# K transposed on VectorE in 32x32 word blocks, q block-diagonal and stationary, pairs of both batches in 16 KB rows

## The chip and the metric

One core of a Trainium2 chip. The metric is the device time of one execution in microseconds; the time before is the median of three runs. The profile shows one execution, taken by the hardware profiler. Engines: TensorE (PE; PEld is its weight load), VectorE (DVE), ScalarE (ACT), GpSimd (POOL) and SyncE (SP), which here only issues transfers; 16 DMA engines move the data.

## What is computed

One decoding step of attention over a sliding window, gated by a small dense block. Cut to what matters:

```python
# x: 2 x 1 x 448; k_cache, v_cache: 2 x 8 x 8192 x 256; wq: 448 x 4096; wo: 4096 x 448; all bf16
xn = layernorm(x)
q = (xn @ wq).reshape(2, 1, 16, 256)            # 16 query heads on 8 K/V heads
k, v = the last 2048 rows of k_cache, v_cache   # per batch and head
p = softmax(q @ k.T * 256 ** -0.5)
s = (p @ v).reshape(2, 1, 4096) @ wo
g = silu(relu(xn @ w1) @ w2)                    # w1: 448 x 1792, w2: 1792 x 448
return x + s * g
```

K and V are 2 x 8 x 2048 x 256 elements each, 16 MB each; wq and wo are 3.5 MB each, w1 and w2 1.5 MB each. Each byte is used once, for one row of q per head, so nearly all the kernel does is to bring K and V in and to turn them into the layout that TensorE wants.

## The kernel before

A pair `k` is one K/V head with both batches (8 pairs); a half is one batch of it, `c = 2k + b`. A half of K or V is one transfer of 1 MB, 128 rows of 8 KB: partition p holds 16 consecutive positions. There are 6 buffers for halves of K and 8 for V.

For the scores the contraction runs over the 256 head elements, so these must lie on partitions, while the transfer puts positions there. `do_T` (L262) therefore transposes K: it reads two bf16 elements as one 4-byte word, transposes four blocks of 128 x 128 words on TensorE into one of three PSUM banks (`tb`), and the bank is copied to a `kt` buffer, by VectorE (L280) and ScalarE (L282) in turn. A pair has 8 such steps. `do_S` (L284) makes the scores of a batch in 8 matmuls with q stationary (4 columns: even or odd head elements, the two heads of the pair) and 512 positions of `kt` streaming, four at a time in column strips of TensorE (`tile_position`). Their lines show as L249, the helper `mm`.

The softmax of a pair: `ch_max` (L300) takes row maxima on VectorE; `ch_rmT` (L305) brings them into one row on TensorE and takes the maximum per head (L309); `ch_bias` (L313) spreads it back over partitions; `ch_exp` (L319) is the exponential on ScalarE with the row sums; `ch_Pt` (L324) transposes P in four TensorE steps and a copy; `ch_sum` (L336) adds the row sums on TensorE with a reciprocal behind it. `do_PV` (L341) multiplies P, stationary in 4 columns, by V, four matmuls of 256 columns at a time. `do_osb` (L355) scales, on VectorE; `do_oT` (L361) turns the result onto partitions and writes it to `at_exp`. At the end `at_exp` is turned into `at2`, 128 small matmuls with `wo` follow (L491), then the gate, the residual and two stores.

The order of work is written out by hand: `steps` is a table of 64 steps, one per `do_T`, into which everything else is put at fixed distances (`at_step`, L435). Every engine executes its own list in that order and waits on semaphores where an operation names what it depends on; so an operation that waits holds all behind it on its engine. The transfers are SP's list, in a fixed order: two halves of K, wq, w1, w2, two halves of K, then V and K in turn (`order`, L462), and wo in five pieces (`WO_PARTS`); a load waits until the transposes (K) or the matmuls (V) that read its buffer last are done. `do_q`, `do_H`, `do_hT` and `do_F` (query, dense block and gate) run once, among the first steps.

## Time and profile before

| | |
|---|---|
| runs | 114.83, 115.55, 116.62 us (median 115.55) |
| profiled execution | 114.63 us, its span 112.8 us |
| busy | PE 81.9, DVE 49.5, ACT 44.5, POOL 1.8 us |
| moved | 44.24 MB, on average 392 GB/s |
| mean granted TensorE clock | 0.884 |

The span goes from the first to the last instruction. The slices of the page cut it in 40 equal parts; PEclk is the clock that TensorE was granted, in tenths, and GB/s is what the transfers moved. The groups of the page and of the view by line give the count of a kind of instruction, its busy time in total and the mean of one in ns, then the idle time of its engine ahead of it and who ended that. The chain that ended last follows the work back from the last instruction, at each step to what released it.

### The profile page before, as it was taken

Reading aid. Unit: us, or ns where it says so; the run is one execution under the profiler, and the core shown is the slowest. Engines: PE = TensorE matmul, PEld = TensorE weight load, DVE = VectorE, ACT = ScalarE, POOL = GpSimd, SP = SyncE. Lnnn points to the kernel's source line nnn. Section 1 sums busy time; section 2 is a strip of 40 time slices with the busy share of each in tenths; the row PEclk is TensorE's granted clock in tenths of the full one; section 3 lists DMA queues with packets and bytes.
Section 4 is the critical chain, followed back from the end, with each engine's and each line's share of the span. In section 5 each row is a group of like instructions: output and inputs, shape, how many; then the busy total and the mean of one; then the engine's idle time right before and its main releaser. Section 6 shows DMA issues by size and latency. Waiting matters only on the chain.

```text
span 112.8 us, 2285 instructions
## 1 busy us (share of the span) xinstructions
PE 81.9 (73%) x990; PEld 51.8 (46%) x990; DVE 49.5 (44%) x131; ACT 44.5 (39%) x57; POOL 1.8 (2%) x13
## 2 busy tenths in 40 slices
PE   0008966005978799999959948998999998675770
PEld 0008952002425476665636526654756664342640
DVE  2038333101125765755826724373665575534201
ACT  0960770000340475666643570367357465020000
POOL 6000000000000000000000000000000000000000
PEclk9999999855589999999999998599999999975555
DMA  2999989999999999999999999999999999999910
GB/s 67 418 483 427 478 346 422 425 423 418 433 412 421 424 418 424 412 421 418 421 418 427 421 418 418 415 421 418 427 415 418 427 424 418 416 422 426 359 58 4
DMA packets 5933, 44.24 MB, mean 392 GB/s; under 512 B 674, under 2 KB 932, under 8 KB 1316
## 3 DMA queue, kind: packets, MB, share of 16 engines
q1 hardware_dynamic: 5896, 44.11, 94.1%
q8 instruction: 7, 0.11, 0.4%
q14 instruction: 2, 0.02, 0.0%
q10 hardware_dynamic: 28, 0.00, 0.0%
HBM read 44.11 MB, written 0.00 MB: 391 GB/s over the span
## 4 chain that ended last, share of the span: by engine, by line
DMA 67%; PE 22%; DVE 4%; SPq 3%; issue 1%; ACT 0%
DMA kbuf<-in_A_k_cache_dram 43%; DMA wqo<-in_A_wo_dram 24%; PE tb L270 9%; PE fbk L249 6%; SPq L36 3%; PE sbk L249 3%; PE obk L249 2%; DVE h_n L406 1%; PE mbk L249 1%; PE mbk L327 1%; DVE tmp L429 1%; DVE kt L280 1%; DVE rm L301 1%; PE mbk L306 0%; DVE tmp L496 0%
## 5 line engine op out<-in xcount | busy, mean ns | idle before, releaser
L270 PE MATMUL tb<-ident_f,kbuf 128*128 128x128 f32 x256 | 43.6, 307 | 10.8 <-DMA kbuf<-in_A_k_cache_dram 10.8
L282 ACT ACTIVATE kt<-tb 128x1024 bf16<-128x1024 bf16 x32 | 32.8, 1024 | 43.8 <-PE tb L270 43.7
L270 PEld LDWEIGHTS tb<-ident_f,kbuf 128*128 128x128 f32 x256 | 31.7, 156 | 19.0 <-DMA kbuf<-in_A_k_cache_dram 11.7
L280 DVE COPY kt<-tb 128x1024 bf16<-128x1024 bf16 x32 | 22.0, 689 | 23.4 <-PE tb L270 23.4
L249 PE MATMUL obk<-vbuf,pt 128*4 128x256 bf16 x256 | 13.0, 292 | 0.0
L249 PE MATMUL sbk<-kt,qz 128*4 128x512 bf16 x128 | 10.4, 401 | 0.0
L357 DVE TENSOR_SCALAR o_sb<-obk,rs 128x256 bf16<-128x256 f32 x16 | 7.5, 471 | 1.6 <-PE obk L249 1.6
L301 DVE TENSOR_REDUCE rm<-sbk 128x1 f32<-128x512 f32 x8 | 5.5, 690 | 5.9 <-PE sbk L249 5.9
L320 ACT ACTIVATE e_sb<-sbk,bias 128x512 bf16<-128x512 f32 x8 | 5.5, 683 | 3.7 <-DVE bias L316 3.7
L249 PE MATMUL mbk<-ident,xg 2*128 2x2 bf16 x7 | 0.3, 163 | 8.9 <-DVE xg L229 8.9
L249 PEld LDWEIGHTS obk<-vbuf,pt 128*4 128x4 bf16 x256 | 4.3, 84 | 5.4 <-issue 3.2
L249 PE MATMUL fbk<-w_sb,xr 128*4 128x448 bf16 x14 | 4.1, 451 | 0.7 <-DVE h_n L406 0.7
L249 PEld LDWEIGHTS mbk<-ident,xg 2*128 2x128 bf16 x7 | 0.3, 100 | 8.9 <-DVE xg L229 8.9
L249 PE MATMUL fbk<-wqo,at 128*2 128x112 bf16 x128 | 3.6, 294 | 0.9 <-issue 0.4
L249 PE MATMUL mbk<-ssum,gsum 128*128 128x1 f32 x16 | 3.2, 270 | 0.6 <-DVE pt L332 0.6
L406 DVE TENSOR_SCALAR h_n<-fbk 4x448 bf16<-4x448 f32 x2 | 1.2, 612 | 5.4 <-PE fbk L249 5.4
L332 DVE COPY pt<-mbk 128x64 bf16<-128x64 bf16 x8 | 1.5, 192 | 4.6 <-PE mbk L327 4.6
L249 PEld LDWEIGHTS fbk<-wqo,at 128*2 128x2 bf16 x128 | 2.8, 118 | 1.6 <-issue 0.6
L327 PE MATMUL mbk<-ident,e_sb 128*128 128x128 bf16 x32 | 3.2, 222 | 0.3 <-ACT e_sb L320 0.3
L249 PEld LDWEIGHTS mbk<-ssum,gsum 128*128 128x128 f32 x16 | 2.7, 212 | 1.3 <-DVE pt L332 0.9
L249 PEld LDWEIGHTS mbk<-one_f,mrow 1*128 1x128 f32 x16 | 2.3, 182 | 2.0 <-DVE mrow L309 2.0
L249 PE MATMUL mbk<-one_f,mrow 1*128 1x1 f32 x16 | 3.0, 256 | 0.3 <-DVE mrow L309 0.3
(65 smaller groups left out, 43.9 us busy)
## 6 DMA issues: line engine op xcount, KB each, us to landing
kbuf<-in_A_k_cache_dram SPq DMA_DIRECT2D x16, 1024.0 KB, 23.0
vbuf<-in_A_v_cache_dram SPq DMA_DIRECT2D x16, 1024.0 KB, 25.2
wqo<-in_A_wq_dram SPq DMA_DIRECT2D x1, 3584.0 KB, 15.0
w_sb<-in_B_w_dram SPq DMA_DIRECT2D x2, 1568.0 KB, 19.7
wqo<-in_A_wo_dram SPq DMA_DIRECT2D x2, 1120.0 KB, 24.3
wqo<-in_A_wo_dram SPq DMA_DIRECT2D x1, 896.0 KB, 27.1
wqo<-in_A_wo_dram SPq DMA_DIRECT2D x2, 224.0 KB, 24.7
x_c<-in_A_x_dram ACTq DMA_DIRECT2D x2, 0.9 KB
```

The lines of the kernel that those rows point to most:

```text
L36: o = _Op(eng, lambda e: e.dma_start(dst, src), [d for d in deps if d is not None], True)
L249: return lambda e: e.matmul(out_ap, lhsT=lhsT, rhs=rhs, start=start, stop=stop, skip_group_check=True, **kw)
L270: o = pr.op(PE, lambda e, n=n, lo=lo: e.matmul(bank_f[:, n * 128:(n + 1) * 128], lhsT=src_f[:, lo:lo + 128], rhs=ident_f[:, :], start=True ...
L280: evac[i] = pr.op(DVE, lambda e: e.tensor_copy(dst[:, :], bank[:, :]), deps)
L282: evac[i] = pr.op(ACTE, lambda e: e.activation(dst[:, :], bank[:, :], ACT.Copy), deps)
L301: st["rm", k] = pr.op(DVE, lambda e: e.tensor_reduce(out=rm[k % 2][:, :], in_=sbk[:, :], axis=AX.X, op=ALU.max), [st["S", k], st.get(("rmT ...
L320: st["exp", k] = pr.op(ACTE, lambda e: e.activation(e_sb[k % 2][:, :], sbk[:, :], ACT.Exp, bias=bias[k % 2][:, 0:1], accum_out=ssum[k % 2] ...
L327: o = pr.op(PE, lambda e, j=j: e.matmul(mb16[:, 512 + 128 * j:640 + 128 * j], lhsT=e_sb[k % 2][:, 128 * j:128 * j + 128], rhs=ident[:, :], ...
L332: st["pt", k] = st["mbk"] = pr.op(DVE, lambda e: e.tensor_copy(view(pt[k % NP], 0, [[16, 4], [4, 4], [1, 4]]), view(mb16, 512, [[128, 4], ...
L357: st["osb", k] = pr.op(DVE, lambda e: e.tensor_scalar(out=o_sb[k % 2][:, cols], in0=obk[k % 2][:, cols], scalar1=rs[:, k:k + 1], scalar2=N ...
L406: st["h_n"] = pr.op(DVE, lambda e: e.tensor_scalar(out=h_n[0:4, u * (FC // 2):(u + 1) * (FC // 2)], in0=fbk[0:4, 0:FC // 2], scalar1=0.0, ...
L429: v_rc = pr.op(DVE, lambda e: e.reciprocal(tmp[:, :], ea[:, :]), [v_d])
```

## The change

The kernel is written anew around another layout:

- A transfer is a whole pair of K or V, 2 MB, in 128 rows of 16 KB: partition 2i + b holds 32 consecutive positions of batch b. There are three buffers for K and three for V. wq, w1 and w2 are issued ahead of the first K.
- `do_T` transposes K on VectorE, in four instructions per pair of 1024 words per partition. Each turns blocks of 32 x 32 words inside a group of 32 partitions.
- What lies in `kt` after that has, on each partition, another word of the head for each of four groups of positions. `do_qbd` therefore lays q out block-diagonally (on GpSimd, 32 partitions at a time), so that 128 stationary columns hold q for the four groups, and `do_S` runs 16 full matmuls of 512 columns per pair, which accumulate in one bank of `sbk` (two banks now).
- P is transposed on VectorE as well (`ch_ptd`), and a product with a mask (`ch_pt`) sorts the batches. `do_PV` runs 16 matmuls of 512 columns per pair with 8 stationary columns, four at a time.
- The bias copy (`ch_bsb`) and the scaling of the output (`do_osb`) move to ScalarE.
- The order is a list: each round transposes pair k in quarters, with the softmax of pair k - 1 and the output of pair k - 2 between them; the last three pairs have their own order. `do_q`, `do_H` and `do_F` come ahead of all rounds.
- wo comes in pieces of 16, 11, 4 and 1 of its 32 rows per partition, the output goes out in one transfer.

```diff
-    NT = W // 128
+    NT = W // 64
+    ROW = NT * DH
...
-    NKB = 6
-    NVB = 8
-    NKT = 12
-    NP = 3
+    NKB = 3
+    NVB = 3
     HC = HD // 2
     FC = DFF // 2
-    WO_PARTS = [10, 10, 8, 2, 2]
+    WO_PARTS = [16, 11, 4, 1]
     NCOL = D // 4
+    QW = 2 * 8 * 128
...
+        ptd = named("ptd", [128, 1024], BF)
+        pt = [named(f"pt{i}", [128, 128], BF) for i in range(2)]
...
-        kt = [named(f"kt{i}", [128, 1024], BF) for i in range(NKT)]
-
...
+        kbuf = [named(f"kbuf{i}", [128, ROW], BF) for i in range(NKB)]
+        vbuf = [named(f"vbuf{i}", [128, ROW], BF) for i in range(NVB)]
+        kt = [named(f"kt{i}", [128, ROW], BF) for i in range(2)]
+
+        sbk = [psum(f"sbk{i}", [128, 512], F32) for i in range(2)]
+        obk = [psum(f"obk{i}", [128, 512], F32) for i in range(2)]
...
-        def kv_src(c, cache):
-            hkv, b = divmod(c, 2)
-            return cache[b, hkv, SK - W:SK, :].rearrange("(p t) d -> p (t d)", t=NT)
...
+        def kv_src(k, cache):
+            return cache[:, k, SK - W:SK, :].rearrange("b (i t) d -> i b (t d)", t=NT)
...
-        def load_k(c):
-            d_k[c] = pr.dma(SP, kbuf[c % NKB][:, :], kv_src(c, A_k_cache), [last_T.get(c - NKB)])
-
-        def load_v(c):
-            d_v[c] = pr.dma(SP, vbuf[c % NVB][:, :], kv_src(c, A_v_cache), [last_PV.get(c - NVB)])
-
-        load_k(0)
-        load_k(1)
+        def load_k(k):
+            d_k[k] = pr.dma(SP, kbuf[k % NKB][:, :], kv_src(k, A_k_cache), [last_T.get(k - NKB)])
+
+        def load_v(k):
+            d_v[k] = pr.dma(SP, vbuf[k % NVB][:, :], kv_src(k, A_v_cache), [last_PV.get(k - NVB)])
+
         d_wq = pr.dma(SP, wqo[:, 0:SLOTS * HC], wq_src)
         d_w1 = pr.dma(SP, w1_sb[:, :], w1_src)
         d_w2 = pr.dma(SP, w2_sb[:, :].rearrange("p (hf f) -> p hf f", hf=2), w2_src)
-        load_k(2)
...
-            v = pr.op(DVE, lambda e: e.tensor_scalar(
-                out=q_n[:, :], in0=obk[0][:, :], scalar1=SCALE, scalar2=None, op0=ALU.mult), [o])
-            deps = [v, v_xr]
...
+            for par in range(2):
+                v = pr.op(DVE, lambda e, par=par: e.tensor_scalar(
+                    out=view(kt[1], 128 * par, [[256, 8], [32, 4], [1, 32]]),
+                    in0=view(obk[0], par, [[64, 8], [0, 4], [2, 32]]),
+                    scalar1=SCALE, scalar2=None, op0=ALU.mult), [o])
+            st["osb", -2] = v
...
+            for h in range(2):
+                for cp in range(8):
+                    n = 8 * h + cp
+                    o = pr.op(PE, mm(nbk[:, 16 * n:16 * n + 16], kt[1][:, 128 * n:128 * n + 128],
+                                     view(ident, 0, [[2, 2], [32, 4], [1, 2]]), h == 0 and cp == 0,
+                                     h == 1 and cp == 7), deps)
...
+        def do_qbd(k):
+            deps = [st["qall"], p_qz, st.get(("S", k - 2))]
+            for a in range(4):
+                st["qbd", k] = pr.op(POOL, lambda e, a=a: e.tensor_copy(
+                    view(qbd[k % 2], 32 * a, [[1024 + 2, 2], [128, 8], [1, 2]], n=32, p0=32 * a),
+                    view(qall, 32 * k, [[16, 2], [2, 8], [1, 2]], n=32, p0=32 * a)), deps)
                 deps = []
...
-                    o = pr.op(PE, mm(fbk[32 * i:32 * i + B, 0:NCOL], h_sb[:, 2 * f:2 * f + 2], w2_sb[:, lo:lo + NCOL],
+                    o = pr.op(PE, mm(fbk[32 * i:32 * i + 17, 0:NCOL], h_sb[:, f:f + 17],
+                                     w2_sb[:, lo:lo + NCOL],
...
+        def do_T(k, n):
+            lo = n * (ROW // 8)
+            src = kbuf[k % NKB][:, :].bitcast(F32)
+            dst = kt[k % 2][:, :].bitcast(F32)
+            deps = [d_k[k], st.get(("S", k - 2)), st["qT"]] if n == 0 else []
+            last_T[k] = pr.op(DVE, lambda e: e.transpose(dst[:, lo:lo + ROW // 8], src[:, lo:lo + ROW // 8]), deps)
+
+        def do_S(k):
+            bank, t = sbk[k % 2], kt[k % 2]
+            deps = [last_T[k], st["qbd", k], st.get(("exp", k - 2))]
...
             for b in range(2):
...
-
-        order = ["v0"] + [n for k in range(2, NPAIR - 2) for n in (f"k{k}", f"v{k - 1}")]
-        order += ["k6", "k7", "v5", "v6", "v7"]
-        loads = []
-        for n in order:
-            load, nb = (load_k, NKB) if n[0] == "k" else (load_v, NVB)
-            loads += [(load, 2 * int(n[1]) + b, nb) for b in range(2)]
-        for i in range(max(steps) + 1):
-            while loads and (loads[0][1] < loads[0][2] or (loads[0][0], loads[0][1] - loads[0][2]) in freed):
-                load, c, _ = loads.pop(0)
-                load(c)
-            for _, fn in sorted(steps.get(i, []), key=lambda a: a[0]):
-                fn()
+                for cp in range(8):
+                    c, par = divmod(cp, 2)
+                    w = (8 * b + cp) * 128
+                    o = pr.op(PE, mm(bank[:, :], qbd[k % 2][:, w:w + 128],
+                                     view(t, 64 * c + 2 * b + par, [[256, NT], [4, 16]]),
+                                     b == 0 and cp == 0, b == 1 and cp == 7), deps)
+                    deps = []
+            st["S", k] = o
+
+        def ch_max(k):
+            st["rm", k] = pr.op(DVE, lambda e: e.tensor_reduce(
+                out=rm[k % 2][:, :], in_=sbk[k % 2][:, :], axis=AX.X, op=ALU.max),
...
+        def ch_rmT(k):
+            st["rmT", k] = pr.op(PE, lambda e: e.matmul(
+                mbk[0:1, 0:128], lhsT=rm[k % 2][:, :], rhs=ident_f[:, :], start=True, stop=True,
+                is_transpose=True), [st["rm", k], p_idf, st.get("mbk")])
+
+        def ch_mrow(k):
+            st["mrow", k] = st["mbk"] = pr.op(DVE, lambda e: e.tensor_reduce(
+                out=view(mrow[k % 2], 0, [[32, 4], [1, 4]], n=1), in_=view(mbk, 0, [[0, 4], [1, 4], [32, 4]], n=1),
+                axis=AX.X, op=ALU.max, negate=True), [st["rmT", k], p_mr, st.get(("bias", k - 2))])
+
+        def ch_bias(k):
+            st["bias", k] = pr.op(PE, mm(mbk[:, 128:129], mrow[k % 2][0:1, :], one_f[0:1, :], True, True),
+                                  [st["mrow", k], p_one, st["mbk"]])
+
+        def ch_bsb(k):
+            st["bsb", k] = st["mbk"] = pr.op(ACTE, lambda e: e.activation(
+                bias[k % 2][:, :], mbk[:, 128:129], ACT.Copy), [st["bias", k]])
+
+        def ch_exp(k):
+            st["exp", k] = pr.op(ACTE, lambda e: e.activation(
+                e_sb[k % 2][:, :], sbk[k % 2][:, :], ACT.Exp, bias=bias[k % 2][:, 0:1],
+                accum_out=ssum[k % 2][:, 0:1]), [st["bsb", k], st.get(("ptd", k - 2)), st.get(("gs", k - 2))])
+
+        def ch_ptd(k):
+            st["ptd", k] = pr.op(DVE, lambda e: e.transpose(
+                ptd[:, :], view(e_sb[k % 2], 0, [[16, NT], [1, 16], [0, 2]])), [st["exp", k], st.get(("pt", k - 1))])
+
+        def ch_pt(k):
+            st["pt", k] = pr.op(DVE, lambda e: e.tensor_tensor(
+                out=view(pt[k % 2], 0, [[4, NT], [1, 4]]), in0=view(ptd, 0, [[32, NT], [1, 4]]),
+                in1=view(pmask, 0, [[0, NT], [1, 4]]), op=ALU.mult), [st["ptd", k], v_pm, last_PV.get(k - 2)])
+
+        def ch_sum(k):
...
+        def do_PV(k):
+            bank, src, p = obk[k % 2], vbuf[k % NVB], pt[k % 2]
+            deps = [d_v[k], st["pt", k], a_z[1], st.get(("osb", k - 2))]
+            for n in range(16):
+                i = n % 4
+                o = pr.op(PE, mm(bank[32 * i:32 * i + 8, :], p[:, 8 * n:8 * n + 8], src[:, 512 * n:512 * n + 512],
+                                 n < 4, n >= 12, tile_position=(0, 32 * i)), deps)
+                deps = []
+            last_PV[k] = o
+
+        def do_osb(k):
+            st["osb", k] = pr.op(ACTE, lambda e: e.activation(
+                o_sb[k % 2][:, :], obk[k % 2][:, :], ACT.Copy, scale=rs[:, k:k + 1]),
+                [last_PV[k], st["rs", k], st.get(("oT", k - 2))])
+
+        def do_oT(k):
+            deps = [st["osb", k], v_fold, st["nbk"]]
+            for dhi in range(2):
+                for t2 in range(2):
+                    lo = 256 * t2 + 128 * dhi
+                    o = pr.op(PE, mm(nbk[:, 4 * dhi:4 * dhi + 4], o_sb[k % 2][:, lo:lo + 128],
+                                     fold[:, 4 * t2:4 * t2 + 4], dhi == 0 and t2 == 0, dhi == 1 and t2 == 1), deps)
+                    deps = []
+            st["oT", k] = o
+
...
+        def add(fn, *a):
+            if 0 <= a[0] < NPAIR:
+                steps.append((fn, a))
+
+        for k in range(NPAIR - 1):
+            c, p = k - 1, k - 2
+            add(do_qbd, k)
+            add(do_T, k, 0)
+            add(ch_max, c)
+            add(ch_rmT, c)
+            add(do_T, k, 1)
+            add(ch_mrow, c)
+            add(ch_bias, c)
+            add(ch_bsb, c)
+            add(ch_exp, c)
+            add(do_osb, p)
+            add(do_T, k, 2)
+            add(do_oT, p)
+            add(do_T, k, 3)
+            add(do_at, p)
+            add(ch_ptd, c)
+            add(ch_pt, c)
+            add(ch_sum, c)
+            add(ch_rs, c)
+            add(do_S, k)
+            if k < NPAIR - 2:
+                add(do_PV, c)
+        x, y, z = NPAIR - 3, NPAIR - 2, NPAIR - 1
+        add(do_qbd, z)
+        for n in range(4):
+            add(do_T, z, n)
+        add(do_S, z)
+        for c in (y, z):
+            add(ch_max, c)
+            add(ch_rmT, c)
+            add(ch_mrow, c)
+            add(ch_bias, c)
+            add(ch_bsb, c)
+            add(ch_exp, c)
+            if c == y:
+                add(do_osb, x - 1)
+                add(do_oT, x - 1)
+                add(do_at, x - 1)
+                add(do_PV, x)
+            add(ch_ptd, c)
+            add(ch_pt, c)
+            add(ch_sum, c)
+            add(ch_rs, c)
+        for k in (x, y, z):
+            if k != x:
+                add(do_PV, k)
+            add(do_osb, k)
+            add(do_oT, k)
+            add(do_at, k)
+
+        order = [("k", 0), ("k", 1)]
+        for k in range(NPAIR - 3):
+            order += [("v", k), ("k", k + 2)]
+        order += [("k", NPAIR - 1)] + [("v", k) for k in range(NPAIR - 3, NPAIR)]
+        loads = list(order)
+
+        def pump():
+            while loads:
+                kind, k = loads[0]
+                done, nb = (last_T, NKB) if kind == "k" else (last_PV, NVB)
+                if k >= nb and (k - nb) not in done:
+                    return
+                loads.pop(0)
+                (load_k if kind == "k" else load_v)(k)
+
+        pump()
+        do_q()
+        do_H(0)
+        do_H(1)
+        do_hT()
+        do_F()
+        for fn, a in steps:
+            fn(*a)
+            if fn is do_PV or (fn is do_T and a[1] == 3):
+                pump()
         assert not loads
 
         d_wo = []
```

221 lines of the change are left out of this document (48 added, 173 removed).

## The prediction, made before the result was known

> **What bounds the kernel now.** I read the page first: the span, the slices and the chain that ended last.
>
> ```profile
> span 112.8 us, 2285 instructions
> PE 81.9 (73%) x990; PEld 51.8 (46%) x990; DVE 49.5 (44%) x131; ACT 44.5 (39%) x57; POOL 1.8 (2%) x13
> PEclk9999999855589999999999998599999999975555
> GB/s 67 418 483 427 478 346 422 425 423 418 433 412 421 424 418 424 412 421 418 421 418 427 421 418 418 415 421 418 427 415 418 427 424 418 416 422 426 359 58 4
> DMA 67%; PE 22%; DVE 4%; SPq 3%; issue 1%; ACT 0%
> ```
>
> The transfers run without a gap from about 2 us to 108 us at a rate that hardly moves, no engine is busy for more than 73% of the span, and 67% of the chain is DMA. TensorE's granted clock (PEclk) is the line to keep in mind: it falls to half in two places and stays there at the end. Next the stages, for the rate by row length (the first stretch is mostly wq with rows of 28 KB, the second only K and V with rows of 8 KB; the last column is GB/s), and the end in order of time:
>
> ```profile
> 7.00:16.00 9.00, 6.79 (x39) 6.55 (x39) 5.30 (x13) 3.69 (x6) 0.00 (x0) 1.00 1.01 433
> 30.00:98.00 68.00, 61.31 (x709) 37.38 (x707) 37.47 (x95) 34.69 (x44) 0.00 (x0) 0.96 1.01 420
> ```
>
> ```profile
> 105.60 2.03 PE L249 MATMUL fbk<-wqo,at 128*2 128x112 bf16 x80 [0.29 <-DVE at L485]
> ...
> 107.93 1.10 PE L249 MATMUL fbk<-wqo,at 128*2 128x112 bf16 x39 [0.30 <-DMA wqo<-in_A_wo_dram]
> ...
> 109.86 0.28 DVE L496 TENSOR_TENSOR tmp<-fbk,g_sb 128x112 f32<-128x112 f32 x1 [4.32 <-PE fbk L249]
> 110.17 0.28 DVE L498 TENSOR_TENSOR out_sb<-tmp,x_c 128x112 bf16<-128x112 f32 x1
> 110.48 0.64 SPq L36 DMA_DIRECT2D out_dram<-out_sb  x1
> ```
>
> The output projection waits for the last pieces of wo, and 4.9 us after 107.93 the span is over. So the kernel is its transfers plus a short end, and compute only has to keep up. The question is whether it still does.
>
> **The change, part by part.**
>
> *Transfers.* The bytes stay; the rows of K and V grow from 8 to 16 KB. By the two rates a row of 8 KB takes 312 ns on one of 16 engines (8192 x 16 / 420) and one of 28 KB 1059 ns; the line through both is 13 ns per row and 27.4 bytes per ns, so 16 KB take 611 ns, 429 GB/s. The 33.6 MB of K and V then need 78.2 us instead of 79.9: 1.7 us less (bounds: 0 at the old rate, 2.4 at 433). That is all the transfers can give. The first slice of the page (67 GB/s over 2.82 us) puts the start of the stream at 2.4. wq, w1 and w2 now go first: 6.9 MB at 433, landed at about 18.5. K pair 0 (2.1 MB) lands at 23.5, and from pair 1 on one follows every 9.8 us (4.2 MB of K and V at 429).
>
> *Removed.* The 256 TensorE transposes, their 64 evacuations and the transposes of P lay under the transfers: nothing is gained on the path.
>
> *VectorE.* A K pair is transposed by four instructions of 1024 words. The trace has no such instruction; these are the nearest rows, with others that the sums below use:
>
> ```profile
> L280 DVE COPY kt<-tb 128x1024 bf16<-128x1024 bf16 x32 | 22.0, 689 | 23.4 <-PE tb L270 23.4
> L301 DVE TENSOR_REDUCE rm<-sbk 128x1 f32<-128x512 f32 x8 | 5.5, 690 | 5.9 <-PE sbk L249 5.9
> L320 ACT ACTIVATE e_sb<-sbk,bias 128x512 bf16<-128x512 f32 x8 | 5.5, 683 | 3.7 <-DVE bias L316 3.7
> L309 DVE TENSOR_REDUCE mrow<-mbk 1x16 f32<-1x64 f32 x8 | 1.6, 203 | 0.4 <-PE mbk L306 0.4
> L320 ACT ACTIVATION_READ_ACCUMULATOR e_sb<-sbk,bias 128x1 f32 x8 | 1.6, 202 | 0.0
> L371 DVE TENSOR_TENSOR at_exp<-fbk,qmask 128x16 bf16<-128x16 f32 x14 | 2.4, 173 | 0.7
> L406 DVE TENSOR_SCALAR h_n<-fbk 4x448 bf16<-4x448 f32 x2 | 1.2, 612 | 5.4 <-PE fbk L249 5.4
> L429 DVE RECIPROCAL tmp<-ea 128x112 f32<-128x112 f32 x1 | 0.9, 853 | 0.0
> ```
>
> The reduce handles 512 four-byte elements in 0.69; against L309's 0.20 for a tiny one, and with most of that 0.20 fixed, an element costs about 1.04 ns, and 1024 words 1.22. The lower bound is the copy: 0.69, as if two words went at once. The upper bound counts a word as two elements: 2.28. I take 1.22, since the reduce is the row with four-byte elements; a pair costs 4.9. The transpose of P (ptd, 1024 two-byte elements) gets the same 1.22.
>
> [...]
>
> *TensorE.* Scores become 16 full matmuls of 512 columns per pair, one after another, where eight ran four at a time. Their price hangs on the clock:
>
> ```profile
> 27.79 1.02 PE L249 MATMUL sbk<-kt,qz 128*4 128x512 bf16 x8
> 29.79 2.60 PE L249 MATMUL fbk<-w_sb,xr 128*4 128x448 bf16 x7
> 33.09 1.49 PE L249 MATMUL fbk<-w_sb,xr 128*4 128x448 bf16 x7 [0.70 <-DVE h_n L406]
> 37.56 0.62 PE L249 MATMUL sbk<-kt,qz 128*4 128x512 bf16 x8
> 39.46 0.27 PE L306 MATMUL mbk<-ident_f,rm 128*1 128x128 f32 x1 [0.69 <-DVE rm L301]
> 40.18 0.38 PE L249 MATMUL mbk<-one_f,mrow 1*128 1x1 f32 x2
> 98.61 0.61 PE L249 MATMUL obk<-vbuf,pt 128*4 128x256 bf16 x16
> 100.20 0.48 PE L249 MATMUL mbk<-ssum,gsum 128*128 128x1 f32 x2 [0.28 <-DVE pt L332]
> 100.74 1.02 PE L249 MATMUL obk<-vbuf,pt 128*4 128x256 bf16 x16
> ```
>
> Eight of the old score matmuls are two rounds of four: 1.02 at half clock, 0.62 at full. The difference, 0.40, is the streaming of 1024 columns at full speed, so a matmul of 512 takes 0.21 (0.42 at half) and about 0.2 is latency paid once. Sixteen in a row: 3.6 at full clock, 7.0 at half. P times V (four rounds of 512 columns) is 1.0 or 1.9. Which clock? The stages cut where the granted clock changed (columns: length, PE busy, PEld, DVE, ACT, POOL, clock, DMA share, GB/s):
>
> ```profile
> 18.48:21.90 3.42, 0.40 (x4) 0.23 (x4) 1.06 (x5) 0.00 (x0) 0.00 (x0) 0.99 0.99 418
> 56.04:59.45 3.41, 2.24 (x32) 1.14 (x28) 1.35 (x2) 1.67 (x3) 0.00 (x0) 1.00 1.00 411
> 66.28:69.69 3.41, 1.66 (x25) 1.01 (x26) 0.69 (x1) 0.98 (x1) 0.00 (x0) 0.99 1.02 420
> 69.69:73.10 3.41, 3.41 (x26) 2.62 (x24) 1.51 (x5) 1.02 (x1) 0.00 (x0) 0.51 1.01 418
> 73.10:76.51 3.41, 3.39 (x39) 1.94 (x41) 2.13 (x6) 2.06 (x3) 0.00 (x0) 1.00 1.01 420
> 96.99:100.41 3.42, 1.99 (x27) 1.21 (x27) 1.85 (x7) 0.78 (x2) 0.00 (x0) 0.99 1.03 428
> 100.41:103.82 3.41, 2.52 (x38) 1.20 (x37) 1.33 (x6) 0.00 (x0) 0.00 (x0) 0.50 1.01 423
> ```
>
> The clock is judged in windows of 3.41 us. One with 1.66 or 1.99 busy is followed by half clock, one with 2.24 is not; at half clock 2.52 busy isn't enough to come back, 3.41 is. Now the new order of work: scores and P times V in one burst of about 4.6 us, then 5 us with only small matmuls (0.27 + 0.38 + 0.48, and oT's four, which I put at 0.4 by these). Wherever the windows fall, one of them has well under 2 us busy, so the clock drops in every pair and the scores start at half. They come back to full at the end of the first window that is full enough. If that means 80% (2.52 is 74%), it ends 0.8 to 1.8 windows after their start, on average 1.3 or 4.4 us, with 65% of the streaming done; the rest takes 1.2 and the latency 0.2: **5.8 us for the scores of a pair** (bounds 3.6 and 7.0).
>
> *The loop of a pair.* VectorE's queue has quarter 0 of the next pair, then the maximum of this one, then quarters 1 to 3. So the three quarters sit behind the maximum, which waits for all scores; and the next scores sit on TensorE behind the row sum (ch_sum), which waits for do_at, queued behind quarter 3. From one pair's last score to the next pair's first: max 0.69, three quarters 3.66, mrow 0.20, the two at 0.35, row sum 0.48, some 0.3 of hand-offs: 5.7. The rest (exp 0.89 with its accumulator read, o_sb on ScalarE, oT) runs beside the quarters, ptd and quarter 0 beside the scores. The loop is 5.7 + 5.8 = **11.5 us, against 9.8 for the transfers**: compute sets the pace, and the gain on the rows is hidden.
>
> The copies added on GpSimd (do_qbd) are free: that engine was busy 1.8 us in all, and they wait only for scores two pairs back. SP's queue holds fewer, longer loads; each K load waits for quarter 3 three pairs back and each V load for P times V three pairs back, and what stands behind waits with it. V of pair 7 waits for P times V of pair 4, behind the scores of pair 5 (96.5 below): about 98.4, landed 5 later, and wo (3.7 MB) at 112, still ahead of its matmuls.
>
> *The start.* Nothing keeps TensorE busy before wq (the transposes that did are gone), so I take half clock: wq lands at 11.1; q 3.2; two scalings of 1024 elements 2.4; sixteen small matmuls about 1.7; H twice 2.60 + 0.61; hT, h_sb and F about 2.0; exp and the gate 1.7, 0.85 of it the reciprocal: 28.8 with hand-offs. All of it is ahead of the first quarter in VectorE's queue, so K pair 0, landed at 23.5, waits 5 us. Transposed at 33.7, scored at 39.5.
>
> *The end.* Six loops, the first 0.5 shorter: scores of pair 6 done at 108.0. Pair 7's quarters, behind ptd and two small operations of pair 5 (1.7 in all), end 0.8 later, and its scores run at the restored clock: 112.4. From there the order is serial: softmax of 6 to its exp 2.4; o_sb, oT, P times V of pair 5 and the row sum 3.5; max and softmax of 7 2.9; o_sb, oT and P times V of 6 and of 7, one after the other, 5.9 at half clock; o_sb, oT, at and the projection's transposes 2.0; 128 output matmuls 3.2 (from 2.03 for 80); two VectorE operations and the store as before, 2.9. That is 22.8, or 20.3 with P times V at full clock; I take 21.5: a span of 133.9.
>
> The sum stands against the profiled execution, 114.63 with a span of 112.8, so 1.83 around it: **135.7 us**. The median shown is 115.55, 0.8% above that execution. A measurement of this kernel tells about 2% from no change.
>
> **Rivals.**
>
> *The clock holds (against me, nearly no change).* If short gaps don't lower the clock, the start ends at 24.3 (q, H and F take 4.5 less), the loop is 5.7 + 3.6 = 9.3, under 9.8, and the transfers set the pace: K pair 6 lands at 77.3, its scores end 1.2 + 5.7 + 3.6 later at 87.8, those of 7 at 94.6, and 20.3 of end give 114.9, **116.7 us**. For it speaks that the window with 2.24 busy kept the clock; against it the drop at 69.69 after a window nearly half busy. [...]
>
> ```profile
> 68.03 0.66 PE L270 MATMUL tb<-ident_f,kbuf 128*128 128x128 f32 x4 [1.83 <-DMA kbuf<-in_A_k_cache_dram]
> ```
>
> *Faster: compute hides.* The one mechanism is a transpose at two words at a time, 0.69 a quarter as in the copy's row. It decides once loop and end shrink by enough: with ptd as well the end loses about 1 us and each loop 1.6, so at a full clock (5.7 - 1.6 + 3.6 = 7.7) pair 7 is scored at about 90 and wo lands last. Then the stream alone counts: 112.8 - 2.4 - 0.3 (four matmuls instead of eight behind the last piece) = 110.1, **112.0 us**. It needs the full clock too: at 5.8 a loop of 9.9 from a late start still ends near 124.
>
> *Transposes at half rate.* At 2.28 the loop is 14.7, pair 0 is scored at 43.7, pair 6 at 131.4, pair 7's quarters end 5.0 later: 161.5 of span, **163 us**. Only the count of bytes speaks for it.
>
> *Rows of 16 KB no faster.* Then 1.7 us of transfers come back, under the compute: 135.7 stays.
>
> **How the numbers follow.** Likeliest 0.62, its own range 124 (clock restored early, quarters short) to 147 (scores at 7.0 throughout); the clock holds 0.13; compute hides 0.13; half rate 0.12. From 113 to 148 lie the likeliest, the second and a little of each other: 0.8. Faster by over 2% (under 112.3) is most of the third: 0.10. Within 2% (to 116.9): the rest of it and half of the second: 0.10. Slower: 0.80.
>
> **What would show it.** Right: PEclk falls to 5 in every pair; one transpose near 1.2 us; the sixteen score matmuls take 5 to 7 us; K is landed before VectorE reaches it; SP waits for VectorE and the transfers show gaps from the middle on; the last wo lands well before the output matmuls. Wrong: PEclk at 9 through the middle, transposes near 0.7, or wo again the last thing waited for.

## The result, and the profile after

The changed kernel took 142.24 us (median of 4 runs, 141.54 to 144.38) against 115.19 us for the kernel before in the same comparison: a ratio of 1.235, with a 95% interval from 1.223 to 1.247. The profiled execution took 141.8 us, with a span of 139.7; the forecast was 135.7 with a span of 133.9.

The page of the changed kernel, its busy times, the slices, the chain and the four groups that matter (count, then busy time and the mean of one in ns, then the idle time ahead):

```profile
span 139.7 us, 1466 instructions
PE 89.4 (64%) x590; PEld 31.7 (23%) x590; DVE 67.7 (48%) x115; ACT 18.9 (14%) x41; POOL 11.8 (8%) x47
PEclk9999977755896896599559959955995999855555
GB/s 156 443 443 374 413 454 422 436 417 436 417 427 441 417 436 427 431 413 431 441 406 431 70 375 417 417 441 155 9 366 422 416 399 39 0 0 0 0 5 1
PE 58%; DVE 22%; ACT 8%; DMA 8%; issue 3%
L244 PE MATMUL sbk<-kt,qbd 128*128 128x512 bf16 x128 | 56.4, 608 | 6.8 <-DVE kt L331 6.8
L331 DVE STREAM_TRANSPOSE kt<-kbuf 128x1024 f32<-128x1024 f32 x32 | 38.0, 1215 | 0.0
L375 DVE STREAM_TRANSPOSE ptd<-e_sb 128x1024 bf16<-128x1024 bf16 x8 | 9.8, 1231 | 1.7 <-ACT e_sb L370 1.7
L244 PE MATMUL obk<-vbuf,pt 128*8 128x512 bf16 x128 | 10.0, 439 | 0.0
```

The chain has turned over: 67% DMA before, 8% now, and 58% TensorE. The transfers run at their old rate and then have holes (slices of 70, 155 and 9 GB/s) and an empty end. The second group down shows the transposes at 1.215 us, where 1.22 was forecast; the first shows 56.4 us in 128 score matmuls, and that is the number to follow. One round in order of time, without the weight loads and GpSimd's copies (start, length, engine, and in brackets the idle time before it):

```profile
43.34 7.07 PE L244 MATMUL sbk<-kt,qbd 128*128 128x512 bf16 x16 [0.45 <-DVE kt L331]
50.34 1.04 PE L244 MATMUL obk<-vbuf,pt 128*8 128x512 bf16 x16
50.45 0.69 DVE L347 TENSOR_REDUCE rm<-sbk 128x1 f32<-128x512 f32 x1 [4.56 <-PE sbk L244]
51.05 1.23 DVE L331 STREAM_TRANSPOSE kt<-kbuf 128x1024 f32<-128x1024 f32 x1
51.30 0.27 PE L352 MATMUL mbk<-ident_f,rm 128*1 128x128 f32 x1
52.21 0.17 DVE L357 TENSOR_REDUCE mrow<-mbk 1x16 f32<-1x64 f32 x1
52.31 2.35 DVE L331 STREAM_TRANSPOSE kt<-kbuf 128x1024 f32<-128x1024 f32 x2
52.44 0.38 PE L244 MATMUL mbk<-one_f,mrow 1*128 1x1 f32 x2 [0.86 <-DVE mrow L357]
53.05 0.69 ACT L370 ACTIVATE e_sb<-sbk,bias 128x512 bf16<-128x512 f32 x1
53.73 0.68 ACT L401 ACTIVATE o_sb<-obk,rs 128x512 bf16<-128x512 f32 x1
54.47 0.27 PE L244 MATMUL nbk<-fold,o_sb 128*128 128x4 bf16 x4 [1.65 <-ACT o_sb L401]
54.77 0.26 DVE L417 TENSOR_TENSOR at_exp<-nbk,qmask 128x16 bf16<-128x16 f32 x2
55.09 0.58 PE L244 MATMUL nbk<-ssum,gsum 128*128 128x1 f32 x2 [0.35 <-DVE at_exp L417]
55.53 7.07 PE L244 MATMUL sbk<-kt,qbd 128*128 128x512 bf16 x16
```

From one start of the scores to the next it is 12.2 us (43.34 to 55.53): 7.07 of scores and 5.1 until the next. The same scores, cut where the granted clock changed (length, busy time and matmuls at work, clock, DMA share, GB/s), and two neighbouring weight loads on either side, one load per matmul:

```profile
43.34:46.40 3.06, 3.06 (x8) 0.50 1.00 428
46.40:50.42 4.02, 4.01 (x10) 1.00 1.01 428
44.62 0.12 PEld L244 LDWEIGHTS sbk<-kt,qbd 128*128 128x128 bf16 x1 [0.30 <-issue]
45.05 0.12 PEld L244 LDWEIGHTS sbk<-kt,qbd 128*128 128x128 bf16 x1 [0.31 <-issue]
47.64 0.11 PEld L244 LDWEIGHTS sbk<-kt,qbd 128*128 128x128 bf16 x1 [0.32 <-issue]
48.07 0.11 PEld L244 LDWEIGHTS sbk<-kt,qbd 128*128 128x128 bf16 x1 [0.32 <-issue]
```

The clock doubles in the middle of the burst and the matmuls don't get faster: the loads start 0.43 us apart on both sides. (The mean of 608 ns in the group is the length of one record; records of neighbouring matmuls overlap, so the price of a burst is read from the distance between starts.) P times V, which follows at the full clock (1.00 from 46.40 to 53.23 us), needs 1.04 us for four rounds of 512 columns, about a quarter of a us each. So something other than the clock holds the scores at 0.43 us a matmul once the clock is full. The prediction had named only the clock.

### The profile page after: what moved, and what is told of

It is laid out like the page before. It is cut to its first block, busy times and chain, and to the rows that moved or that the text cites. A ratio compares the mean times of both kernels' runs of the same rounds, so it can differ in the third digit from the quotient of the medians.

```text
span 139.7 us, 1466 instructions
## 1 busy us (share of the span) xinstructions
PE 89.4 (64%) x590; PEld 31.7 (23%) x590; DVE 67.7 (48%) x115; ACT 18.9 (14%) x41; POOL 11.8 (8%) x47
## 4 chain that ended last, share of the span: by engine, by line
PE 58%; DVE 22%; ACT 8%; DMA 8%; issue 3%
PE sbk L244 40%; DVE kt L331 10%; DMA wqo<-in_A_wq_dram 8%; PE fbk L244 6%; PE obk L244 5%; PE nbk L244 4%; ACT o_sb L401 4%; ACT e_sb L370 3%; DVE rm L347 3%; PE mbk L244 2%; DVE ptd L375 2%; DVE kt L266 2%; DVE at_exp L417 1%; ACT bias L366 1%; DVE h_n L298 1%
## 5 line engine op out<-in xcount | busy, mean ns | idle before, releaser
L244 PE MATMUL sbk<-kt,qbd 128*128 128x512 bf16 x128 | 56.4, 608 | 6.8 <-DVE kt L331 6.8
L331 DVE STREAM_TRANSPOSE kt<-kbuf 128x1024 f32<-128x1024 f32 x32 | 38.0, 1215 | 0.0
L244 PEld LDWEIGHTS sbk<-kt,qbd 128*128 128x128 bf16 x128 | 15.2, 123 | 42.7 <-issue 35.6
L286 POOL COPY qbd<-qall 32x32 bf16<-32x32 bf16 x32 | 6.6, 205 | 87.1 <-PE sbk L244 72.8
L375 DVE STREAM_TRANSPOSE ptd<-e_sb 128x1024 bf16<-128x1024 bf16 x8 | 9.8, 1231 | 1.7 <-ACT e_sb L370 1.7
L244 PE MATMUL nbk<-fold,o_sb 128*128 128x4 bf16 x36 | 2.3, 169 | 12.6 <-ACT o_sb L401 11.5
L244 PE MATMUL obk<-vbuf,pt 128*8 128x512 bf16 x128 | 10.0, 439 | 0.0
L401 ACT ACTIVATE o_sb<-obk,rs 128x512 bf16<-128x512 f32 x9 | 6.1, 680 | 5.5 <-PE obk L244 5.5
L244 PE MATMUL nbk<-ssum,gsum 128*128 128x1 f32 x16 | 4.1, 322 | 3.9 <-ACT e_sb L370 2.1
L244 PE MATMUL obk<-wqo,xr 128*4 128x512 bf16 x28 | 3.2, 624 | 3.7 <-DMA wqo<-in_A_wq_dram 3.7
L244 PEld LDWEIGHTS nbk<-ssum,gsum 128*128 128x128 f32 x16 | 3.4, 263 | 4.9 <-ACT e_sb L370 2.3
## 6 DMA issues: line engine op xcount, KB each, us to landing
wqo<-in_A_wo_dram SPq DMA_DIRECT2D x1, 112.0 KB, 14.0
```

The costliest lines, as they stand in the source:

```text
L244: return lambda e: e.matmul(out_ap, lhsT=lhsT, rhs=rhs, start=start, stop=stop, skip_group_check=True, **kw)
L286: st["qbd", k] = pr.op(POOL, lambda e, a=a: e.tensor_copy(view(qbd[k % 2], 32 * a, [[1024 + 2, 2], [128, 8], [1, 2]], n=32, p0=32 * a), vi ...
L331: last_T[k] = pr.op(DVE, lambda e: e.transpose(dst[:, lo:lo + ROW // 8], src[:, lo:lo + ROW // 8]), deps)
L375: st["ptd", k] = pr.op(DVE, lambda e: e.transpose(ptd[:, :], view(e_sb[k % 2], 0, [[16, NT], [1, 16], [0, 2]])), [st["exp", k], st.get(("p ...
L401: st["osb", k] = pr.op(ACTE, lambda e: e.activation(o_sb[k % 2][:, :], obk[k % 2][:, :], ACT.Copy, scale=rs[:, k:k + 1]), [last_PV[k], st[ ...
```

## The experiments

A time without a ratio is that of a single execution.

**Theories.** A: the scores are slow because the moving operand of a score matmul has a step of four elements (8 bytes), so that 512 columns take 0.43 us at any clock, twice their price at the full one. B, the prediction's: the clock does it. For the 5.1 us between the scores there were two theories as well: three quarters of the transposes lie on the path (the prediction), or only one.

**Adjacent columns** (e1_contig). The matmul reads 512 neighbouring columns of `kt` (other columns than the scores need, the same number):

```diff
-view(t, 64 * c + 2 * b + par, [[256, NT], [4, 16]])
+t[:, 512 * (8 * b + cp):512 * (8 * b + cp) + 512]
```

> The score matmuls stream 512 adjacent columns of kt instead of every fourth element; so the scores are not those of the reference, the work is the same in number and size. Theory A (step): a step of 8 bytes in the moving operand holds a matmul of 512 columns at 0.43 us whatever the clock. Then a matmul takes 0.21 here wherever the granted clock is full and 0.43 where it is half, the scores of a pair 4 to 6.5 us, and the time falls from 142 to 128 to 136. Theory B (clock, as predicted): the price was the half clock alone; then nothing changes, 0.43 and 142. Theory C (the load of 128 stationary columns is not hidden): nothing changes either, 0.43 and 142, also where the clock is full.

125.62 us. In order of time, two rounds:

```profile
51.40 5.30 PE L244 MATMUL sbk<-kt,qbd 128*128 128x512 bf16 x16
61.61 5.30 PE L244 MATMUL sbk<-kt,qbd 128*128 128x512 bf16 x16
```

The scores fell from 7.07 to 5.30, the span by 16.1 us, and the group of scores by 16.0 (56.4 to 40.4): the fall of the span is that of the scores. The time is 2.4 us under the range of theory A. Theory B, and theory C of the expectation, had the time unchanged; the weight loads are as before here. Adjacent columns also do away with the pieces of 16 in which the pattern comes; e2_word4 below keeps these and changes the step alone.

**The clock kept up** (e3_warm). Matmuls on unused data in the waits, four behind `ch_rmT` and seven behind `ch_bias`, with the step of 8 bytes left as it is:

```diff
             add(ch_rmT, c)
+            steps.append((warm, (4,)))
...
             add(ch_bias, c)
+            steps.append((warm, (7,)))
```

> Eleven matmuls of 512 columns whose result nobody reads are put on TensorE in each round, four behind the transposed maximum and seven behind the bias, in the gap between two pairs' scores. Both theories expect the granted clock to stay full from the first rounds on. Theory B (clock): scores of a pair fall from 7.0 to 3.6 us, the loop of a pair from 12.1 to 9, the time to 117 to 121. Theory A (step): the scores stay at 6.9 to 7.0 and the time at 140 to 145.

143.75 us. The page's clock, and a round:

```profile
PEclk9999999997799999999999999999999999755558
57.47 7.07 PE L245 MATMUL sbk<-kt,qbd 128*128 128x512 bf16 x16
```

Full clock and still 7.07, and a time within the 140 to 145 of theory A: theory B falls.

**Both together** (e5_contig_warm).

> Adjacent columns as the moving operand (scores not the reference's) and 11 matmuls on unused data per round that keep TensorE's clock up. Theory: step and clock each have a share in the scores, the larger wins; with both gone a score matmul takes 0.21-0.23 us, the sixteen 3.6, gap and scores 8.6, so the transfers (9.8 a pair) set the pace; some 20 of end: 114 to 118 us. Rival: what was left with adjacent columns (0.33 us each, 5.3 for sixteen) is a pace of the matmuls themselves and not the clock: scores 5.3 again and 126 to 128 us.

118.95 us, 1 us above the range given.

```profile
50.00 3.61 PE L245 MATMUL sbk<-kt,qbd 128*128 128x512 bf16 x16
75.55 3.62 PE L245 MATMUL sbk<-kt,qbd 128*128 128x512 bf16 x16
85.83 3.62 PE L245 MATMUL sbk<-kt,qbd 128*128 128x512 bf16 x16
L332 DVE STREAM_TRANSPOSE kt<-kbuf 128x1024 f32<-128x1024 f32 x32 | 38.0, 1216 | 4.5 <-DMA kbuf<-in_A_k_cache_dram 4.4
```

3.6 is what the prediction had worked out for sixteen matmuls at the full clock. So the clock has its share once the step is gone: 5.30 with the clock swinging (0.82 on average over the run), 3.62 with it held (0.97 from 30 to 98 us), and the rival of the expectation (5.3 again) falls. Up to 75 us a round takes 8.5; the next one takes 10.3 because VectorE waits for K, as in the last row: compute has caught up with the transfers.

**A wider step** (x_stride16).

```diff
-view(t, 64 * c + 2 * b + par, [[256, NT], [4, 16]])
+view(t, 32 * c + 2 * b + par, [[256, NT], [8, 16]])
```

> The moving operand's step doubled from 4 to 8 elements, 16 bytes (other columns, so the scores are not the reference's). Theory one, the price follows the bytes that are passed over: 0.87 us a matmul, 13.9 for sixteen, some 7 more per pair, near 197 us. Theory two, any step over 4 bytes costs the same: 0.433, time unchanged at 139 to 143 us.

208.29 us; the group of the scores, and a burst with the P times V behind it:

```profile
L244 PE MATMUL sbk<-kt,qbd 128*128 128x512 bf16 x128 | 116.3, 1077 | 6.4 <-DVE kt L331 6.3
52.89 14.56 PE L244 MATMUL sbk<-kt,qbd 128*128 128x512 bf16 x16
67.38 1.88 PE L244 MATMUL obk<-vbuf,pt 128*8 128x512 bf16 x16
```

The sixteen take 14.56 us, 0.90 from start to start (the 1077 ns are again the length of one record): about twice the 0.43 of 8 bytes, and near the 0.87 and 13.9 of theory one, while theory two falls. One thing limits the comparison. The profile recorded no change of the granted clock in this run and so gives it as 1.000, but P times V takes 1.88 us, where in the changed kernel it took 1.04 at the full clock above and 1.88 at a granted 0.50 (at 127.15 us), so I take it that TensorE ran at half clock here. What a step of 16 bytes costs at the full clock is not shown. The small matmuls in the gaps are slower as well (a matmul of `one_f` into `mbk` lasts 357 ns on average, against 268 in the changed kernel), which is part of the 11 us between 197 and 208.

**The order in the gap** (e4_order). All four quarters of the next pair ahead of the maximum:

```diff
-            add(do_T, k, 0)
+            for n in range(4):
+                add(do_T, k, n)
             add(ch_max, c)
             add(ch_rmT, c)
-            add(do_T, k, 1)
             add(ch_mrow, c)
...
-            add(do_T, k, 2)
...
-            add(do_T, k, 3)
```

> All four quarters of the next pair's transpose go ahead of the maximum in VectorE's queue; nothing else changes. Theory of the prediction (three quarters on the path between one pair's scores and the next): the gap of 5.2 us loses most of 3.5, the loop falls from 12.1 to about 9, the time to 122 to 126. Rival, read from the chain of the changed kernel (only quarter 1 is on it, ahead of mrow; the rest of the gap is the softmax, the output scaling, oT, at and the row sum in series): the gap loses about 0.9, the time falls by 5 to 6, to 136 to 138.

138.82 us.

```profile
54.12 7.07 PE L244 MATMUL sbk<-kt,qbd 128*128 128x512 bf16 x16
65.62 7.06 PE L244 MATMUL sbk<-kt,qbd 128*128 128x512 bf16 x16
```

The gap is 4.4 us (61.19 to 65.62) instead of 5.1, not some 3 less. That is the rival's mechanism, with a little less gained than its 0.9 a round and a time 0.8 us above its range. Only one quarter lay on the path, and the round shown above tells which: it stands between the row maximum and `mrow` (51.05 to 52.28). The other two run beside bias, exponential and `o_sb`, which are needed anyway before the row sum.

**A step of 4 bytes, paid by VectorE** (e2_word4). The transposes write each block with the batches apart, so that a score matmul reads neighbouring words:

```diff
-dst[:, lo:lo + ROW // 8]
+view(dst.tensor, lo, [[32, ROW // 256], [1, 16], [16, 2]])
...
-view(t, 64 * c + 2 * b + par, [[256, NT], [4, 16]])
+view(t, 64 * c + 32 * b + par, [[256, NT], [2, 16]])
```

> The transpose writes the two batches of a block apart, so that the scores step 4 bytes instead of 8; the rest is as in the changed kernel. Theory A, with a limit by what a fetch brings of use: 0.21 per matmul at full clock, scores of a pair 4 to 6.5 us, 128 to 136 us in all, and the rest of the time is then the clock's. If any step over adjacent elements costs the double, 0.43 and 142. Theories B and C: 0.43 and 142. The transposes stay at 1.22 if the order of their writes costs nothing.

147.35 us, slower than the changed kernel. Below the two groups, weight loads of one burst: two of its first part, and the last eight:

```profile
L332 DVE STREAM_TRANSPOSE kt<-kbuf 128x1024 f32<-128x1024 f32 x32 | 57.7, 1871 | 0.0
L244 PE MATMUL sbk<-kt,qbd 128*128 128x512 bf16 x128 | 46.0, 535 | 12.4 <-DVE kt L332 12.4
61.82 0.14 PEld L244 LDWEIGHTS sbk<-kt,qbd 128*128 128x128 bf16 x1 [0.28 <-issue]
62.24 0.14 PEld L244 LDWEIGHTS sbk<-kt,qbd 128*128 128x128 bf16 x1 [0.28 <-issue]
63.95 1.62 PEld L244 LDWEIGHTS sbk<-kt,qbd 128*128 128x128 bf16 x8 [0.28 <-issue]
```

The scores give back 10.4 us in all (56.4 to 46.0), and the transposes, 1.87 instead of 1.22 us for the same words in another order, take 19.7. One quarter, of 1.87, lies in the gap, and TensorE now waits 12.4 us for them. For the scores the run says more than its time does: with the columns still in pieces of 16 and only the step halved, the loads start 0.43 us apart (61.82 to 62.24) and over the last eight some 0.21 (1.62 in all): by the kernel before (1.02 us for two rounds of four at 0.50, 0.62 at 1.00, also at a step of 4 bytes) the prices of half and full clock. The run's mean clock is 0.82. So at half clock a step of 8 bytes costs no more than one of 4; what it takes away is the gain of the full clock.

**Batches on the two halves of the partitions** (e6_halves, and e7_order2 with another order of work). A block of 32 partitions then holds one batch, and the step is 4 bytes without permuted writes:

```diff
-rearrange("b (i t) d -> i b (t d)", t=NT)
+rearrange("b (i t) d -> b i (t d)", t=NT)
...
-view(t, 64 * c + 2 * b + par, [[256, NT], [4, 16]])
+view(t, 4096 * b + 64 * c + par, [[256, 16], [2, 32]])
```

> Batches on the lower and upper half of the partitions instead of on even and odd ones, the whole result computed: a score matmul then reads its 512 columns at a step of 4 bytes, the transposes write as before, P is transposed in 512 elements instead of 1024. Theory (the step of 8 bytes is what the scores cost): 5.3 to 5.8 for the scores with the clock swinging as before, transposes still 1.22, ptd 0.65, gap about 4.6, loop 9.9 to 10.3: 121 to 126 us. Rival (a step of 4 bytes costs too): scores near 7, 138 us or more.

> As e6_halves, with another order: scores of a pair in two halves, the first after two quarters of the transposes, with the row maximum of the pair before between them on TensorE; the next pair's quarters around the softmax; K pair 0 ahead of w1 and w2, the dense block behind the first scores; the last pairs in the same pipeline as all others. Theory: nothing of the layout holds the kernel above its transfers; about 9.8 a pair, wo landed last: 111 to 114 us. Rival (compute still holds it up, a loop over 10 or an end over 17): 117 us or more.

662.16 and 667.39 us: both expectations fell, over a thing that none of the theories had. From 30 to 150 us of e6_halves (PE, PEld, DVE, ACT, POOL, clock, DMA share, GB/s):

```profile
30.00:150.00 120.00, 14.66 (x53) 5.26 (x53) 11.04 (x14) 0.95 (x3) 1.63 (x8) 0.54 0.13 54
L339 DVE STREAM_TRANSPOSE kt<-kbuf 128x1024 f32<-128x1024 f32 x32 | 38.0, 1219 | 452.1 <-DMA kbuf<-in_A_k_cache_dram 452.1
```

54 GB/s is an eighth of 428 (53.5), and a DMA share of 0.13 is about two sixteenths: the same 128 rows, with the batch as the outermost dimension, give work to about two of the 16 engines at a time. The outermost dimension is 2 here and 64 in the changed kernel and in the next run, where the share is 1.01; how the rows are shared out is not shown beyond that.

**One transfer per batch** (e8_halves2, and e9_order2 with the other order).

```diff
-d_k[k] = pr.dma(SP, kbuf[k % NKB][:, :], kv_src(k, A_k_cache), [last_T.get(k - NKB)])
+d_k[k] = [pr.dma(SP, kbuf[k % NKB][64 * b:64 * b + 64, :], s, [last_T.get(k - NKB)])
+          for b, s in enumerate(kv_src(k, A_k_cache))]
```

> As e6_halves, with each pair of K or V brought in by two transfers of 64 rows, one per batch, instead of one whose outer dimension is the batch. Theory: what made e6_halves slow was that such a transfer used 2 of the 16 engines (54 GB/s against 430); with 64 rows as the outer dimension all 16 work and the expectation of e6_halves stands: scores 5.3 to 5.8, loop 9.9 to 10.3, 121 to 126 us. Rival: two transfers of 1 MB into half of the partitions each are slower than one of 2 MB over all: under 300 GB/s, 150 us or more.

> As e7_order2 with the transfers of e8_halves2. Theory: nothing is left that holds the kernel above its transfers; 9.8 a pair, wo landed last at about 106, 5 to 8 of work behind it: 111 to 115 us, 1 to 4% under the kernel before. Rival (compute still holds it up): 117 us or more.

189.38 and 189.34 us (e9_order2: 1.654 times the kernel before, 1.642 to 1.666). The rival of e8_halves2 held (e9_order2 lies in the range of its own, 117 us or more, but it is the transfers and not compute that hold it up):

```profile
30.00:150.00 120.00, 54.11 (x242) 21.91 (x242) 47.66 (x77) 8.59 (x23) 4.91 (x24) 0.66 1.01 216
```

All engines are busy (1.01), at 216 GB/s instead of 428: two transfers of 64 rows, each into 64 neighbouring partitions, move at half the rate. The 1 MB of a transfer is not the reason, since the kernel before moves 1 MB at a time at 420 GB/s; 64 rows spread over all 128 partitions were not run. So whether the 64 rows or the 64 neighbouring partitions halve the rate is not shown. Batches on even and odd partitions, as the changed kernel has them, avoid both losses (428 GB/s) and pay for it with the step of 8 bytes.

**Both batches streaming together** (p2_pen_order). The transfers stay as in the changed kernel. All 32 columns of a block stream, at a step of 4 bytes; q of both batches is stationary, in rows of their own, and one more matmul of two rows adds -1000 where the batches differ, so that the exponential is zero there:

```diff
+pr.op(PE, mm(bank[:, :], pen[0:2, :], view(ident, 0, [[0, 256], [1, 2]], n=2), True), ...)
...
-view(t, 64 * c + 2 * b + par, [[256, NT], [4, 16]])
+view(t, 4096 * u + 64 * c + par, [[256, 16], [2, 32]])
```

The order changes too: K pair 0 ahead of w1 and w2, the dense block beside the first two pairs, the scores in two halves, the last pairs in the same pipeline as the others.

> Batches on even and odd partitions as in the changed kernel, one transfer of 128 rows per pair, and the whole result computed, but the columns of both batches stream together at a step of 4 bytes: each score matmul has q of both batches stationary, and one more matmul of two rows adds -1000 where batch of q and batch of K differ. P is then transposed in 512 elements and P times V reads it as it lies. The order is that of e7_order2, with the first half of the dense block ahead of the first scores. Theory (step and order are all that put the changed kernel over its transfers): scores 4 to 5.8 with the extra matmul, transfers 400 GB/s or more without gaps, wo landed last at 104 to 107, 4 to 5 behind it: 110 to 114 us, 1 to 4% under the kernel before. Rival (compute still holds it up somewhere, gaps in the transfers): 117 us or more.

114.00 us against 114.49: ratio 0.9945, 0.9911 to 0.9978, the upper edge of the expectation.

```profile
GB/s 165 329 484 398 405 432 427 418 438 452 411 435 429 429 435 411 441 405 447 417 435 420 435 423 423 429 417 435 429 435 435 423 417 429 419 424 416 357 35 1
L335 DVE STREAM_TRANSPOSE kt<-kbuf 128x1024 f32<-128x1024 f32 x32 | 37.8, 1220 | 7.5 <-DMA kbuf<-in_A_k_cache_dram 7.5
L248 PE MATMUL sbk<-kt,qbd 128*128 128x512 bf16 x128 | 38.1, 448 | 2.3 <-DVE kt L335 2.3
105.65 3.17 PE L248 MATMUL fbk<-wqo,at 128*17 128x112 bf16 x128 [0.32 <-DVE at L503]
```

No hole in the transfers any more, and VectorE waits for K. But the projection starts behind `at`, not behind wo. The theory for that, which the next run puts to the test: the last two pairs still wait for one another.

**The last pairs** (p3_order3). The softmax of the pair before is put between the quarters of the transposes and of the scores; P times V goes ahead of the next pair's first quarter, and the row sums get a bank of their own. The three were not run apart. The first of them, against p2_pen_order and in part:

```diff
-            add(do_S, k, 0)
+            add(do_S, k, 0, 0)
             add(ch_max, c)
             add(ch_rmT, c)
+            add(do_T, k, 2)
             add(ch_mrow, c)
+            add(do_S, k, 0, 1)
             add(ch_bias, c)
+            add(do_T, k, 3)
```

> As p2_pen_order, in another order: the row maximum, its row and the bias of the pair before lie between the quarters of the transposes and the quarters of the scores of the pair at work, P is transposed and P times V issued before the next pair's first quarter, and the row sums have a bank of their own. Theory (in p2_pen_order the transfers end at about 106 but the projection's input is ready only at 105.4, because the last two pairs wait for one another): scores of pair 7 end at 90 to 93 instead of 96.9, the projection follows the last pieces of wo, span 109 to 110, 111 to 113 us. Rival (the end was not held up by the order of the last pairs): 113.5 to 114.5 us as p2_pen_order.

113.32 us against 114.42: ratio 0.9913, 0.9889 to 0.9936.

```profile
93.71 1.93 PE L249 MATMUL sbk<-kt,qbd 128*128 128x512 bf16 x8 [0.73 <-DVE kt L336]
103.68 1.68 PE L249 MATMUL fbk<-wqo,at 128*17 128x112 bf16 x64 [0.32 <-DVE at L504]
106.22 1.75 PE L249 MATMUL fbk<-wqo,at 128*17 128x112 bf16 x64 [0.86 <-DMA wqo<-in_A_wo_dram]
```

The scores of pair 7 end at 95.6, later than the 90 to 93 expected, yet the second half of the projection now waits for wo, as in the kernel before. The time lies between the theory's 111 to 113 and the rival's 113.5 to 114.5, so neither range held. This version is 0.9% under the kernel before; the interval leaves out 1, but the difference is smaller than the 2% that the prediction asks for to tell a change. The new layout without the new order was not run with working transfers, so how the 28 us between the changed kernel and p2_pen_order divide among step, half-size transposes of P and order stays open; e1_contig gives the step alone 16.

## Why the prediction was right, and where it was not

- **What bounds it.** Right: compute sets the pace, and the transfers get holes. SP's longest wait for VectorE was 26.3 us.
```profile
SPq L36 <- DVE kt L331: 36.5, 2, 26.3
```
- **Transposes.** 1.215 us against 1.22, and `ptd` 1.231 against 1.22. The row of the four-byte reduce was the right neighbour; neither bound (0.69, 2.28) came true, and with them fall the rivals of a faster transpose and of half rate.
- **Rows of 16 KB.** 428 GB/s in the stretch shown, against 429 worked out; under compute it brought nothing, as said.
- **The start.** First scores begun at 31.96 and done at 39.03, against 33.7 and 39.5: 1.7 earlier in, 0.5 earlier out. Half clock was right for q (3.15 us against 3.2, and 1.68 in the kernel before, although PEclk reads 9 there, ahead of the first clock change that was recorded), but not for the two H, which took 1.86 and 2.36 instead of 2.60 each.
- **The scores: the step that failed.** "5.8 us for the scores of a pair" by the clock was 7.07, or 7.06, in each of the first seven. The clock did swing as foretold (PEclk falls to 5 again and again), and with adjacent columns the swinging clock gave 5.30, near the 5.8. The steps of 3.41 us are those of the kernel before (there half clock from 21.88 to 32.11 and 69.66 to 73.08): half clock from 25.92 to 36.16, 42.99 to 46.40 and 53.23 to 60.05, and it ended at 46.40 after a window with 3.06 us busy. That the clock is judged in such windows is my reading of these stretches. But the row that the price was taken from (0.21 us per matmul of 512 columns) was of an operand read at a step of 4 bytes, and the new operand's step of 8 was not priced at all. It lies in the diff, as `[4, 16]` in the view. The 0.42 for half clock was right; the 0.21 for the full clock is what the step ruled out. That is 1.27 us more per pair, and 6.9 for pair 7, whose scores were to run at 3.6 at the restored clock.
```profile
103.84 13.97 PE L244 MATMUL sbk<-kt,qbd 128*128 128x512 bf16 x32
```
- **The gap: nearly the right sum from the wrong parts.** 5.7 was forecast and 4.9 to 5.1 measured (4.3 in the first round). Not three quarters of the transposes are on the path but one; in the place of the two others stand the bias and its copy, which the sum left out, and exponential, `o_sb` and `oT`, which I had put "beside the quarters". A queue says what may not overtake, not what is late; I had added up VectorE's list and not followed the other engines to the row sum.
- **Together.** A loop of 12.0 to 12.2 instead of 11.5 (11.4 instead of 11.0 for the first) puts the end of pair 6's scores at 110.9 instead of 108.0; pair 7's took 6.9 instead of 4.4 and ended at 117.8 instead of 112.4; the end took 21.9 instead of 21.5. That is the 5.8 us between the spans of 133.9 and 139.7. Part of the nearness is luck: for scores at 7.0 throughout the prediction itself gave 147, and the shorter gaps and the earlier start took some 5 us of it back.
- **The clock holds (rival).** It did not hold: it fell at 42.99 us after a window with 1.03 of 3.41 us busy, as in the kernel before at 69.69 after one whose longest idle stretch was 1.83 (the row of 68.03). And e3_warm shows that it would not have helped: with the clock held, 143.75 and not 116.7, because at the step of 8 bytes the scores still took 7.07, where adjacent columns took 3.62.
- **Compute hides (rival).** Its 112.0 was the price of the transfers alone. p3_order3, where they set the pace, comes to 113.32, 1.1 us under the kernel before instead of the 2.6 that the rival gave.

## What to carry to other kernels

Price a matmul by a row whose moving operand is read with the same step, or treat the step as unknown and bound it: the count of columns and the clock are not enough (512 columns at the full clock took 0.43 us here, 0.22 adjacent). When operands are laid out anew, follow the layout through transfer, transposes and matmul together; here each place that got the fast order moved the cost to another (1.22 to 1.87 us on VectorE, half or an eighth of the rate in the transfers), and of the layouts run, only streaming both batches and masking left all three fast. To find what lies between two bursts, follow the chain across engines from the later one back, rather than add up one engine's queue.

## What the runs showed of the hardware

- A matmul of 512 bf16 columns in a burst of sixteen took about 0.22 us with adjacent columns and the clock kept up (e5_contig_warm: 3.62 for sixteen, 0.97 granted from 30 to 98 us), and as much at a step of 4 bytes in p3_order3 (1.93 for eight, 0.90 granted from 30 to 98 us). At a step of 8 bytes it took 0.43 at either clock (changed kernel: 7.07 for sixteen, across 0.50 and 1.00), and at 16 bytes 0.90 (x_stride16: 14.56 for sixteen), at half clock by the 1.88 us of P times V. At a step of 4 bytes and half clock it is 0.42, worked out from the kernel before (1.02 us for two rounds of four at 0.50), and the 0.43 between loads in e2_word4 agrees.
- In x_stride16 P times V took the same 1.88 us as at a granted 0.50 in the changed kernel, although the bursts of matmuls lasted 14.56 us.
- A VectorE transpose of 1024 four-byte words per partition took 1.22 us (changed kernel: 1215 ns), and 1.87 with the same words written in the order of even and odd columns (e2_word4: 1871 ns).
- 128 rows of 16 KB moved at 428 GB/s with 64 as the outer dimension (changed kernel, 43.34 to 46.40 us), at 54 with 2 (e6_halves), and at 216 when 64 of them at a time went to one half of the partitions (e8_halves2).
